# Attention's output product as four products on row halves of the array, in place of two block diagonal ones

## The chip, the cores and the metric

One core of one Trainium2 chip runs one program. TensorE (PE) multiplies, loading the stationary operand (PEld) and streaming the moving one; VectorE (DVE), ScalarE (ACT) and GpSimd (POOL) work beside it; SyncE (SP) issues DMAs. The metric is the device time of one execution in microseconds, as the median of several runs.

## The reference

Three parts follow each other; the output of one is the input of the next.

```python
# 1. attention over 32 memory slots: 4 batches, 8 heads, 576 tokens, 64 wide
a = softmax(phi, axis=2)                          # (4, 8, 576, 32)
k_m = einsum('bhsm,bhsd->bhmd', a, k)             # (4, 8, 32, 64)
v_m = einsum('bhsm,bhsd->bhmd', a, v)
attn = softmax(q @ k_m^T / 8, axis=-1)            # (4, 8, 576, 32)
x = (attn @ v_m) as (2304 tokens, 512)
# 2. mixture of 8 experts, two for each token
noisy = x @ w_gate + log1p(exp(x @ w_noise)) * noise
out = sum over a token's two experts of weight * (relu(x @ w1[e]) @ w2[e])   # 512 -> 1024 -> 512
# 3. two layers
h = out @ w_in                                    # 512 -> 2048
result = (h * cos(h)) @ w_out                     # 2048 -> 512
```

## The kernel before

**Attention.** The 2304 tokens are 18 tiles of 128 rows (`NT`). For each of the 4 batches `k_gen(b)` takes the softmax over phi, sums k and v into 32 slots a head (`kp`, L589), normalises them (`kd`, `vm`) and lays out two operands. `bdkt` holds the slot keys for the score product. `bdv` (L608) holds the slot values: for a group g of four heads, 128 rows (4 heads of 32 slots) and 272 columns. Columns 0 to 255 are block diagonal: head j's 64 values stand in columns 64 j to 64 j + 63 of its own 32 rows and the rest is zero, which POOL makes with the mask `bmask` (L612). Columns 256 to 271 are each slot's values times that head's rows of the two gate matrices (`pw`, L623, copied by ACT at L624). So one product gives a tile's attention output and its 16 gate logits (8 for the gate, 8 for the noise).

For each tile `t_gen(t)` computes the scores (`sc`, L659, PE), the softmax (`smx` and `sd` on DVE, the exponential on ACT, `ssm` on DVE, `d` on POOL), transposes `d` on PE (`pt`, L679), copies it to `e2T` on ACT (L681), and multiplies on PE (L689): for g = 0 and 1, `x[:, g, 0:272]`, one PSUM bank for each g. All operands are fp32; each such product is two records in the profile. ACT copies columns 0 to 255 of both banks to `xs` with a scale (L694) and columns 256 to 271 to the tile's place in `lgb` (L700), then makes the fp16 high part of `xs` (L704); POOL subtracts it for the low part (L705) and SP stores both (L706). There is one buffer for `x`, so a tile's product waits for ACT's copies of the tile before. A tile that spans two batches (tiles 4 and 13; `segs`) is computed in two halves of 64 tokens, each with its batch's operand.

**Routing.** Tiles 0 to 7 are group 0 and tiles 8 to 17 group 1. `route(g)` first adds the two partial logits of `lgb` (L349, DVE), then goes through noise, the two largest, ranks (`rank`, PE) and a table product (`tab`, L433, PE, behind the last tile's product x) to the row indices `idxA` (L438) and `idxB`. Steps of `route(0)` stand between the steps of tiles 12, 13, 14 and 17 in DVE's order; `route(1)` follows the last tile.

**Experts and last layers.** POOL gathers rows of x by `idxA` (L829), SP transposes them, and PE multiplies by w1 and w2 for the 8 experts and then by the last two layers: fp16 products `h`, `y`, `g`, `o`, from 106 us to the end. ACT and DVE scale the weights to fp16 high and low parts meanwhile, the first expert's already during the attention's end (`w`, `junk`, L219).

**Order.** Each step is put in a list with a time written by hand (`at`, `a_of(i) = 21 + 2.5 i`, `t_steps`, `k_steps`); a planner turns times into priorities and orders each engine's instructions by them and by a simulated timeline. Some places in the order are fixed by hand, as in

```python
AHEAD = (9, 10, 11, 13, 14, 15, 16)
with gated(f"t{ahead}T"):     # product x of tile t behind the transposes of tile t + 1 on PE
with gated(f"t{ahead}E"):     # copy of x of tile t behind the copy e2T of tile t + 1 on ACT
with gated(f"t{NT - 1}P"):    # table products behind the last product x
```

Of the kernel before, what the change touches and what calls it, by code (L numbers as in the profile page):

```python
# [9 lines left out]
F32 = mybir.dt.float32  # L10
# [4 lines left out]
AF = mybir.ActivationFunctionType  # L15
OP = mybir.AluOpType
AX = mybir.AxisListType
PSUM = bass.MemoryType.PSUM

P = 128  # L20
B, H, S, D, M = 4, 8, 576, 64, 32
# [3 lines left out]
E = 8  # L25
# [4 lines left out]
GROUPS = [(0, 8), (8, 18)]  # L30
# [30 lines left out]
def fused_kernel(ctx, tc, phiT, qT, kv, wgn, noise, w1, w2, wi, wo, out):  # L61
    nc = tc.nc
    V, A, G, T, SP = nc.vector, nc.scalar, nc.gpsimd, nc.tensor, nc.sync
# [15 lines left out]
    last = {}  # L79
# [25 lines left out]
    def sm(shape, dt, name):  # L105
        return small.tile(shape, dt, name=name)
# [32 lines left out]
    hp = sm([P, 1], F32, "hp")  # L139
    V.memset(hp, math.pi / 2)  # L140

    bmask = sm([P, 4], F32, "bmask")
    V.memset(bmask, 0.0)
    for j in range(4):
        V.memset(bmask[32 * j:32 * j + 32, j:j + 1], 1.0)
    wgn_sb = sm([64, H, 2 * E], F32, "wgn_sb")
    noise_sb = sm([P, NT, E], F32, "noise_sb")
    lgb = {}
    sT = sm([P, 2, NT], F32, "sT")
# [192 lines left out]
    def route(g):  # L342

        t0, t1 = GROUPS[g]
        n = t1 - t0
        ts = slice(t0, t1)
        u, w1p, l, c, y = (rg(g, k, n, E) for k in "uwlcy")
        lgp = rg(g, "lgp", n, 2 * E)
        V.tensor_tensor(lgp, lgb[g][:, :, 0], lgb[g][:, :, 1], op=OP.add)  # L349
        gate, z = lgp[:, :, 0:E], lgp[:, :, E:]  # L350
        last["u"] = V.scalar_tensor_tensor(u, z, -1.0, z, op0=OP.mult, op1=OP.max)
        A.activation(u, u, AF.Exp, scale=-1.0)
# [30 lines left out]
        d = rg(g, "d", n)  # L383
# [37 lines left out]
        for t in range(t0, t1, 3):  # L421
# [6 lines left out]
            for q in range(m):  # L428
                ohp = small.tile([P, 2, P], F16, tag="ohp", name="ohp", bufs=4)
                for k in range(2):  # L430
                    V.tensor_scalar(ohp[:, k], iota_r, pf[:, t + q, k:k + 1], None, op0=OP.is_equal)
                    with gated(f"t{NT - 1}P"):
                        last[f"tab{t + q - t0}"] = T.matmul(  # L433
                            tb[:, :nc_], lhsT=ohp[:, k], rhs=oha[:, q, k], start=(t + q == t0 and k == 0),
                            stop=(t + q == t1 - 1 and k == 1))
# [80 lines left out]
    ap = att.enter_context(tc.tile_pool(name="ap", bufs=2))  # L516
# [37 lines left out]
    def k_gen(b):  # L554
# [50 lines left out]
        last[f"bdk{b}V"] = V.tensor_copy(bk[0:64, :, 0:M], pv[0:64, :, 0, :])  # L605
        last[f"bdk{b}A"] = A.activation(bk[64:128, :, M:], pv[64:128, :, 1, :], AF.Copy)
        yield
        bv = ap.tile([P, 2, 272], F32, tag="bdv", name="bdv")  # L608
        bdv[b] = bv
        mb = bmask[:, :, None].to_broadcast([P, 4, D])  # L610
        for g in range(2):
            G.tensor_tensor(bv[:, g, 0:256].rearrange("p (j d) -> p j d", d=D),  # L612
                            vm[:, g, None, :].to_broadcast([P, 4, D]), mb, op=OP.mult)
        pv = trk("pv")
        for g in range(2):
            T.transpose(pv[0:64, g * P:(g + 1) * P], vm[:, g, :], ident)
# [4 lines left out]
        for h in range(H):  # L621
            r = slice(32 * (h % 4), 32 * (h % 4) + 32)
            T.matmul(pw[r, h // 4, :], lhsT=vt[:, h // 4, r], rhs=wgn_sb[:, h, :], start=True, stop=True)  # L623
        A.activation(bv[:, :, 256:272], pw, AF.Copy)  # L624
        yield
        vq = ap.tile([P, 1], F32, tag="vq", name="vq", bufs=1)
        sb = ap.tile([P, 2], F32, tag="sb", name="sb", bufs=1)
# [25 lines left out]
    def t_gen(t):  # L653

        sc = scb[:, t % 2]
        for p0, n, b in segs(t):
            c0 = (t % 8) * P + p0
            for c in range(4):
                T.matmul(sc[p0:p0 + n, 64 * c:64 * c + 64], lhsT=qt[t // 8][:, c, c0:c0 + n],  # L659
                         rhs=bdkt[b][:, c, :], start=True, stop=True)  # L660
        yield
        sv = sc.rearrange("p (h m) -> p h m", m=M)
        mx = ap.tile([P, H], F32, tag="smx", name="smx")
        V.tensor_reduce(mx, sv, axis=AX.X, op=OP.max)
        dk = sds[t % 4]
        dv = dk[:, :, 0:M]
        V.tensor_tensor(dv, sv, mx[:, :, None].to_broadcast([P, H, M]), op=OP.subtract)
        yield
        A.activation(dv, dv, AF.Exp, scale=0.125)
        yield  # L670
        su = ap.tile([P, H], F32, tag="ssm", name="ssm")
        V.tensor_reduce(su, dk, axis=AX.X, op=OP.add)
        last[f"t{t}V"] = V.reciprocal(su, su)
        d = ap.tile([P, 2 * P], F32, tag="d", name="d")
        G.tensor_tensor(d.rearrange("p (h m) -> p h m", m=M), dv, su[:, :, None].to_broadcast([P, H, M]), op=OP.mult)
        yield
        pt = ptb[:, t % 2]
        for g in range(2):
            last[f"t{t}T"] = T.transpose(pt[:, g * P:(g + 1) * P], d[:, g * P:(g + 1) * P], ident)  # L679
        eT = ap.tile([P, 2, P], F32, tag="e2T", name="e2T")  # L680
        last[f"t{t}E"] = A.activation(eT.rearrange("p g s -> p (g s)"), pt, AF.Copy)  # L681
        yield
        ahead = t + 1 if t in AHEAD else None
        x = aps.tile([P, 2, 512], F32, tag="x", name="x")
        with gated(f"t{ahead}T"):
            for p0, n, b in segs(t):
                pn = slice(p0, p0 + n)
                for g in range(2):
                    last[f"t{t}P"] = T.matmul(x[pn, g, 0:272], lhsT=eT[:, g, pn], rhs=bdv[b][:, g, :], start=True,  # L689
                                              stop=True)  # L690
        yield
        xs = l2k([P, DM], F32, "xs")
        with gated(f"t{ahead}E"):
            A.activation(xs.rearrange("p (g d) -> p g d", g=2), x[:, :, 0:256], AF.Copy,  # L694
                                          scale=sT[:, 0, t:t + 1])
        g = ROUTE_OF[t]
        if t == GROUPS[g][0]:
            n = GROUPS[g][1] - GROUPS[g][0]
            lgb[g] = rg(g, "lgb", n, 2, 2 * E)
        last[f"t{t}A"] = A.activation(lgb[g][:, t - GROUPS[g][0]], x[:, :, 256:272], AF.Copy)  # L700
        yield
        hl = l2k([P, 2 * DM], F16, "hl")
        hv = hl.rearrange("p (w d) -> p w d", w=2)
        A.activation(hv[:, 0], xs, AF.Copy)  # L704
        G.tensor_tensor(hv[:, 1], xs, hv[:, 0], op=OP.subtract)  # L705
        SP.dma_start(xd[t * P:(t + 1) * P, :], hl)  # L706
        yield
# [403 lines left out]
    x = X[0]  # L1111
# [161 lines left out]
```

## Time and profile before

| | |
|---|---|
| time of 3 runs | median 925.77 us (924.71 to 926.04) |
| profiled execution | 926.95 us, its span 925.1 us |
| PE, PEld busy | 879.5 us (95%), 511.0 us (55%) |
| DVE, ACT, POOL busy | 582.4 (63%), 467.7 (51%), 215.4 (23%) |
| mean granted clock of TensorE | 0.974 of 2.4 GHz |

Times are microseconds from the start of the span. Busy PE time is modelled and runs from a product's start to its last result, so products that follow each other overlap in it; intervals between starts tell more. In a timeline each row merges equal instructions that follow each other: start, time from the first start to the last end, engine, line, operation, output and inputs, the part of the array used and the shape, count, and in brackets the idle time of the engine before it with what ended it. `PEclk` 1.00 is 2.4 GHz and 0.50 is 1.2 GHz.

### The profile page before, as it was taken

The page shows a single profiled execution, that of the slowest core. Times are in us where ns is not written, and L with a number is a line of the kernel's source. Part 1 is how long each engine was busy: PE and PEld are TensorE (multiplying, and loading weights), DVE is VectorE, ACT ScalarE, POOL GpSimd, SP SyncE. Part 2 cuts the span into 40 slices and gives each one's busy share as a digit, 9 for nine tenths or more (in the row PEclk, how much of TensorE's full clock was granted, in tenths as well). Part 3 has the DMA queues.
Part 4 walks back from the last instruction along what each step waited for, and adds up shares of the span by engine and source line. Part 5 has one row for each costly group of instructions (what it writes and reads, how often), then busy time and mean ns, then how long its engine had stood idle before and what let it go on. Part 6 is the DMA issues. An engine that isn't in the chain of part 4 may idle for free. (4 is left out here: it accounts for less than half of the span.)

```text
span 925.1 us, 14179 instructions
## 1 busy us (share of the span) xinstructions
PE 879.5 (95%) x5368; PEld 511.0 (55%) x5368; DVE 582.4 (63%) x1266; ACT 467.7 (51%) x830; POOL 215.4 (23%) x234
## 2 busy tenths in 40 slices
PE   5997499999999999999999998999999999999997
PEld 4875355746566574756555565664444444444564
DVE  3668753766657575766571377787875765554564
ACT  3588426666666676777761334444333432422242
POOL 1355222110201101020000034434322521322221
PEclk9897599999999999999999999999999999999999
DMA  9982469787778979696762553322301610200010
GB/s 353 395 300 86 114 167 263 240 291 236 237 257 252 289 242 282 231 307 247 205 216 93 171 160 58 95 52 72 80 1 12 149 23 12 68 12 1 1 46 23
DMA packets 108246, 146.55 MB, mean 158 GB/s; under 512 B 65808, under 2 KB 66448, under 8 KB 106128
## 3 DMA queue, kind: packets, MB, share of 16 engines
q1 hardware_dynamic: 89536, 103.56, 36.5%
q0 software_dynamic: 6080, 19.93, 7.5%
q10 hardware_dynamic: 12560, 22.13, 6.7%
q8 instruction: 43, 0.70, 0.3%
q14 instruction: 27, 0.22, 0.1%
HBM read 95.26 MB, written 35.13 MB: 141 GB/s over the span
## 5 line engine op out<-in xcount | busy, mean ns | idle before, releaser
L219 PE MATMUL h<-x,w 128*128 128x384 f16 (+1 forms) x1536 | 215.3, 302 | 9.8 <-DMA x<-xg 9.2
L219 PE MATMUL y<-w,hT 128*128 128x512 f16 x960 | 210.7, 379 | 2.2 <-issue 2.2
L219 PE MATMUL g<-x2T,win 128*128 128x256 f16 (+1 forms) x1152 | 203.8, 327 | 5.5 <-DVE ty L1048 4.9
L219 PE MATMUL o<-wout,gT 128*128 128x512 f16 x864 | 202.5, 380 | 0.3 <-POOL gT L1050 0.2
L219 PEld LDWEIGHTS <-w 128*128 128x128 f16 x1536 | 151.5, 99 | 68.9 <-DMA x<-xg 8.8
L219 PEld LDWEIGHTS <-win 128*128 128x128 f16 x1152 | 113.2, 98 | 89.8 <-issue 6.8
L219 PEld LDWEIGHTS <-hT 128*128 128x128 f16 x960 | 93.9, 99 | 111.4 <-issue 2.7
L1050 POOL TENSOR_TENSOR gT<-ty,gT 128x256 f16<-128x256 f32 (+1 forms) x96 | 92.9, 968 | 253.8 <-ACT gT L1049 249.9
L1047 ACT ACTIVATE tt<-tt,hp 128x256 f32<-128x256 f32 (+1 forms) x96 | 58.9, 614 | 163.8 <-DVE tt L1046 147.7
L219 PEld LDWEIGHTS <-gT 128*128 128x128 f16 x864 | 84.4, 98 | 93.8 <-POOL gT L1050 1.9
L219 DVE SCALAR_TENSOR_TENSOR w<-raw,wsc,w 128x1024 f16<-128x1024 f32 x64 | 81.1, 1288 | 32.8 <-ACT w L219 31.2
L219 DVE SCALAR_TENSOR_TENSOR hT<-h,hT 128x384 f16<-128x384 f32 (+1 forms) x128 | 61.4, 487 | 61.9 <-ACT hT L219 61.7
L1044 DVE SCALAR_TENSOR_TENSOR ty<-g,wis,bct 128x256 f32<-128x256 f32 (+1 forms) x96 | 58.9, 613 | 65.1 <-PE g L219 65.1
L219 ACT ACTIVATE hT<-h 128x384 f16<-128x384 f32 (+1 forms) x128 | 55.2, 435 | 74.3 <-PE h L219 70.2
L1048 DVE SCALAR_TENSOR_TENSOR ty<-g,fac,tt 128x256 f32<-128x256 f32 (+1 forms) x96 | 59.1, 616 | 53.0 <-ACT tt L1047 52.5
L1049 ACT ACTIVATE gT<-ty 128x256 f16<-128x256 f32 (+1 forms) x96 | 50.2, 523 | 66.0 <-DVE ty L1048 65.9
L829 POOL DMA_INDIRECT xg<-xd,idxB x24 | 25.1, 1045 | 218.3 <-DMA x<-xg 206.9
L219 ACT ACTIVATE w<-raw,wsc 128x1024 f16<-128x1024 f32 x64 | 71.6, 1140 | 4.1 <-DVE wsc L219 1.9
L219 ACT ACTIVATE junk<-raw 128x1024 bf16<-128x1024 f32 x64 | 67.3, 1052 | 3.8 <-ACT o L219 2.5
L1046 DVE SCALAR_TENSOR_TENSOR tt<-tt,ty 128x256 f32<-128x256 f32 (+1 forms) x96 | 67.5, 703 | 2.6
L219 ACT ACTIVATE o<-y,ysc 128x512 f32<-128x512 f32 x40 | 27.5, 687 | 73.3 <-PE y L219 73.3
L968 POOL DMA_INDIRECT y<-yd,sidx x36 | 36.2, 1004 | 88.4 <-DMA yd<-o 80.7
(234 smaller groups left out, 712.8 us busy)
## 6 DMA issues: line engine op xcount, KB each, us to landing
raw<-in_w SPq DMA_DIRECT2D x32, 1024.0 KB, 11.4
yd<-o ACTq DMA_DIRECT2D x40, 256.0 KB, 6.8
kvt<-in_kv SPq DMA_DIRECT2D x9, 1024.0 KB
cvt<-in_wi SPq DMA_DIRECT2D x8, 1024.0 KB
wst<-cvt SPq DMA_DIRECT2D x16, 512.0 KB
cvt<-in_wo SPq DMA_DIRECT2D x8, 1024.0 KB, 8.6
yd<-zero ACTq DMA_DIRECT2D x13, 512.0 KB, 7.1
xd<-hl SPq DMA_DIRECT2D x18, 256.0 KB, 2.0
```

The costliest lines, as they stand in the source:

```text
L219: last[key] = fn(*a, **kw)
L829: G.indirect_dma_start(out=g, out_offset=None, in_=xd[0:NA * P] if part == 0 else xd, in_offset=bass.IndirectOffsetOnAxis(ap=idx[:, col:co ...
L968: G.indirect_dma_start(out=y, out_offset=None, in_=yd[0:rows], in_offset=bass.IndirectOffsetOnAxis(ap=sidx[:, t, k:k + 1], axis=0))
L1044: V.scalar_tensor_tensor(y, ph[:, :n], wis[:, 2 * E + c:2 * E + c + 1], bct[j], op0=OP.mult, op1=OP.mult)
L1046: V.scalar_tensor_tensor(t, t, MAGIC, y, op0=OP.subtract, op1=OP.subtract)
L1047: A.activation(t, t, AF.Sin, bias=hp, scale=-2.0 * math.pi)
L1048: V.scalar_tensor_tensor(y, ph[:, :n], fac[:, c:c + 1], t, op0=OP.mult, op1=OP.mult)
L1049: A.activation(g[:, 0, :n], y, AF.Copy)
L1050: G.tensor_tensor(g[:, 1, :n], y, g[:, 0, :n], op=OP.subtract)
```

## The change

The mask gets two columns in place of four, so that `bdv` has 128 + 16 = 144 columns: a head's values stand in the first or the second 64 columns by its number's parity. Rows 0 to 63 (heads 0 and 1 of the group) and rows 64 to 127 (heads 2 and 3) are then separate products of 64 rows: `x[:, j, 144 g : 144 g + 144]` for row half j, so that the two row halves of a group go to two PSUM banks and the two groups lie side by side in a bank. Each product gives 128 columns of x and a partial sum of the 16 logits. ACT's copy of x reads four pieces of 128 columns, its copy to `lgb` four pieces of 16, and `route` reduces four partial sums in place of adding two. `lgb` of group 0 moves to the attention's pool.

```diff
--- before.py
+++ after.py
@@ -139,10 +139,10 @@
     hp = sm([P, 1], F32, "hp")
     V.memset(hp, math.pi / 2)
 
-    bmask = sm([P, 4], F32, "bmask")
+    bmask = sm([P, 2], F32, "bmask")
     V.memset(bmask, 0.0)
     for j in range(4):
-        V.memset(bmask[32 * j:32 * j + 32, j:j + 1], 1.0)
+        V.memset(bmask[32 * j:32 * j + 32, j % 2:j % 2 + 1], 1.0)
     wgn_sb = sm([64, H, 2 * E], F32, "wgn_sb")
     noise_sb = sm([P, NT, E], F32, "noise_sb")
     lgb = {}
@@ -346,7 +346,7 @@
         ts = slice(t0, t1)
         u, w1p, l, c, y = (rg(g, k, n, E) for k in "uwlcy")
         lgp = rg(g, "lgp", n, 2 * E)
-        V.tensor_tensor(lgp, lgb[g][:, :, 0], lgb[g][:, :, 1], op=OP.add)
+        V.tensor_reduce(lgp, lgb[g].rearrange("p t s n -> p t n s"), axis=AX.X, op=OP.add)
         gate, z = lgp[:, :, 0:E], lgp[:, :, E:]
         last["u"] = V.scalar_tensor_tensor(u, z, -1.0, z, op0=OP.mult, op1=OP.max)
         A.activation(u, u, AF.Exp, scale=-1.0)
@@ -605,12 +605,12 @@
         last[f"bdk{b}V"] = V.tensor_copy(bk[0:64, :, 0:M], pv[0:64, :, 0, :])
         last[f"bdk{b}A"] = A.activation(bk[64:128, :, M:], pv[64:128, :, 1, :], AF.Copy)
         yield
-        bv = ap.tile([P, 2, 272], F32, tag="bdv", name="bdv")
+        bv = ap.tile([P, 2, 144], F32, tag="bdv", name="bdv")
         bdv[b] = bv
-        mb = bmask[:, :, None].to_broadcast([P, 4, D])
+        mb = bmask[:, :, None].to_broadcast([P, 2, D])
         for g in range(2):
-            G.tensor_tensor(bv[:, g, 0:256].rearrange("p (j d) -> p j d", d=D),
-                            vm[:, g, None, :].to_broadcast([P, 4, D]), mb, op=OP.mult)
+            G.tensor_tensor(bv[:, g, 0:128].rearrange("p (j d) -> p j d", d=D),
+                            vm[:, g, None, :].to_broadcast([P, 2, D]), mb, op=OP.mult)
         pv = trk("pv")
         for g in range(2):
             T.transpose(pv[0:64, g * P:(g + 1) * P], vm[:, g, :], ident)
@@ -621,7 +621,7 @@
         for h in range(H):
             r = slice(32 * (h % 4), 32 * (h % 4) + 32)
             T.matmul(pw[r, h // 4, :], lhsT=vt[:, h // 4, r], rhs=wgn_sb[:, h, :], start=True, stop=True)
-        A.activation(bv[:, :, 256:272], pw, AF.Copy)
+        A.activation(bv[:, :, 128:144], pw, AF.Copy)
         yield
         vq = ap.tile([P, 1], F32, tag="vq", name="vq", bufs=1)
         sb = ap.tile([P, 2], F32, tag="sb", name="sb", bufs=1)
@@ -686,18 +686,25 @@
             for p0, n, b in segs(t):
                 pn = slice(p0, p0 + n)
                 for g in range(2):
-                    last[f"t{t}P"] = T.matmul(x[pn, g, 0:272], lhsT=eT[:, g, pn], rhs=bdv[b][:, g, :], start=True,
-                                              stop=True)
+                    for j in range(2):
+                        pj = slice(64 * j, 64 * j + 64)
+                        last[f"t{t}P"] = T.matmul(x[pn, j, 144 * g:144 * g + 144], lhsT=eT[pj, g, pn],
+                                                  rhs=bdv[b][pj, g, :], start=True, stop=True)
         yield
         xs = l2k([P, DM], F32, "xs")
         with gated(f"t{ahead}E"):
-            A.activation(xs.rearrange("p (g d) -> p g d", g=2), x[:, :, 0:256], AF.Copy,
-                                          scale=sT[:, 0, t:t + 1])
+            xv = x[:, :, 0:288].rearrange("p j (g n) -> p g j n", g=2)
+            A.activation(xs.rearrange("p (g j d) -> p g j d", g=2, j=2), xv[:, :, :, 0:128], AF.Copy,
+                         scale=sT[:, 0, t:t + 1])
         g = ROUTE_OF[t]
         if t == GROUPS[g][0]:
             n = GROUPS[g][1] - GROUPS[g][0]
-            lgb[g] = rg(g, "lgb", n, 2, 2 * E)
-        last[f"t{t}A"] = A.activation(lgb[g][:, t - GROUPS[g][0]], x[:, :, 256:272], AF.Copy)
+            if g:
+                lgb[g] = rg(g, "lgb", n, 4, 2 * E)
+            else:
+                lgb[g] = ap.tile([P, n, 4, 2 * E], F32, name="lgb", bufs=1)
+        last[f"t{t}A"] = A.activation(lgb[g][:, t - GROUPS[g][0]].rearrange("p (g j) n -> p g j n", g=2),
+                                      xv[:, :, :, 128:144], AF.Copy)
         yield
         hl = l2k([P, 2 * DM], F16, "hl")
         hv = hl.rearrange("p (w d) -> p w d", w=2)
```

## Rows read from the trace of the kernel before

**Rows 1.** Busy time by stages: stretch, length, each engine's busy time (count), clock, DMA.
```profile
30.10:63.00 32.90, 32.71 (x388) 26.86 (x388) 20.29 (x64) 26.64 (x78) 16.49 (x22) 1.00 1.02 379
...
74.40:77.90 3.50, 2.68 (x19) 1.95 (x19) 3.47 (x18) 2.25 (x5) 1.43 (x2) 1.00 0.19 75
77.90:81.30 3.40, 1.72 (x10) 0.98 (x7) 3.30 (x12) 3.07 (x8) 2.07 (x3) 1.00 0.28 108
81.30:93.00 11.70, 8.20 (x29) 4.98 (x26) 7.98 (x34) 8.98 (x20) 5.83 (x6) 0.50 0.22 83
```

**Rows 2.** Timeline of PE around the product x of a whole tile.
```profile
31.28 0.38 PE L679 MATMUL pt<-ident,d 128*128 128x128 f32 x2
31.50 1.08 PE L689 MATMUL x<-bdv,e2T 128*128 128x272 f32 x4
32.42 0.38 PE L577 MATMUL et<-ident,ew 128*128 128x128 f32 x2
32.63 1.00 PE L659 MATMUL sc<-bdk,qt 128*128 128x64 f32 x8
33.48 0.83 PE L577 MATMUL et<-ident,ew 128*128 128x128 f32 x6
```

**Rows 3.** Timeline of PE around the product x of tile 4, in two halves.
```profile
46.30 0.39 PE L601 MATMUL pk<-ident,kd 128*128 128x128 f32 x2
46.61 1.14 PE L689 MATMUL x<-bdv,e2T 128*64 128x272 f32 x8
47.69 0.44 PE L679 MATMUL pt<-ident,d 128*128 128x128 f32 x2
47.96 0.38 PE L577 MATMUL et<-ident,ew 128*128 128x128 f32 x2
```

**Rows 4.** Waits of PE from 63 to 93 us: total, times, longest.
```profile
PE sc L659 <- DVE sd L667: 2.6, 3, 1.2
```

**Rows 5.** Timeline of PE at the attention's end.
```profile
84.19 2.02 PE L689 MATMUL x<-bdv,e2T 128*128 128x272 f32 x4
86.00 0.64 PE L679 MATMUL pt<-ident,d 128*128 128x128 f32 x2
87.13 2.18 PE L689 MATMUL x<-bdv,e2T 128*128 128x272 f32 x4 [0.50 <-ACT rt L700]
90.24 2.18 PE L689 MATMUL x<-bdv,e2T 128*128 128x272 f32 x4 [0.92 <-ACT rt L700]
92.22 0.47 PE L433 MATMUL tab<-oha,ohp 128*128 128x40 f16 x8
```

**Rows 6.** Timeline of ACT at the attention's end.
```profile
86.31 0.69 ACT L694 ACTIVATE xs<-x,sT 128x512 f32<-128x512 f32 x1 [0.97 <-PE x L689]
...
89.41 0.69 ACT L694 ACTIVATE xs<-x,sT 128x512 f32<-128x512 f32 x1 [0.51 <-PE x L689]
...
92.52 0.69 ACT L694 ACTIVATE xs<-x,sT 128x512 f32<-128x512 f32 x1 [0.78 <-PE tab L433]
...
94.22 0.63 ACT L704 ACTIVATE hl<-xs 128x512 f16<-128x512 f32 x1
```

**Rows 7.** Timeline of all engines, from the last tile to the first expert product.
```profile
94.98 1.16 POOL L705 TENSOR_TENSOR hl<-xs,hl 128x512 f16<-128x512 f32 x1 [1.96 <-issue]
...
96.31 1.93 POOL L829 DMA_INDIRECT xg<-xd,idxA  x1 [0.17 <-issue]
...
106.43 5.30 PE L219 MATMUL h<-x,w 128*128 128x256 f16 x24 [8.71 <-DMA x<-xg]
```

**Rows 8.** DVE's groups by form: busy time, mean ns, idle before.
```profile
L559 DVE TENSOR_REDUCE mx<-ph 128x2 f32<-128x1152 f32 x1 | 1.3, 1301 | 0.0
L349 DVE TENSOR_TENSOR rlgp<-rlgb 128x128 f32<-128x128 f32 x1 | 1.2, 1219 | 0.0
```

**Rows 9.** Timeline of DVE at the first index result.
```profile
94.37 0.31 DVE L349 TENSOR_TENSOR rt<-rt 128x160 f32<-128x160 f32 x1
...
95.30 0.17 DVE L438 TENSOR_SCALAR idxA<-tab 128x16 int32<-128x16 f32 x1 [0.23 <-PE tab L433]
```

## The prediction

> **What bounds the kernel now.** I read the busy table by stages first, then PE's timeline through the attention, then who waits for whom there, then ACT, DVE and POOL at the attention's end. The change touches only the first 95 us. From 30.1 to 63 us PE is busy 32.71 of 32.90 us at the full clock, with ACT at 26.64 and DVE at 20.29 [rows 1]: PE sets the pace, its products start back to back, and no wait of PE's is listed in that stretch. From 74.4 to 81.3 us DVE is busy 3.47 of 3.50 and 3.30 of 3.40 us while PE has slack [rows 1], and PE's score products wait for DVE's subtraction (2.6 us) [rows 4]: DVE sets the pace. From 81.3 to 93 us TensorE runs at its lower level, 1.2 GHz [rows 1], and the last tiles go round one loop: product x on PE, its copy by ACT out of the only x buffer, the next product x. ACT stands idle 0.97, 0.51 and 0.78 us ahead of the last three copies [rows 6], and the last two products start after idle times of 0.50 and 0.92 us ending at ACT's copy [rows 5]. What follows is a chain in series: ACT's fp16 copy of tile 17 at 94.22 [rows 6], POOL's difference at 94.98, the first gather of expert rows at 96.31, and the first expert product at 106.43, for which PE had waited 8.71 us [rows 7]. From there to the end PE is nearly always busy, so what the attention gives back moves the end by as much.
>
> **The product itself.** A full tile has four records of 272 columns (two fp32 passes for each of two products), from 31.50 to the next product's start at 32.42: 0.92 us, 229 ns each [rows 2]. After the change it has eight of 144 columns, 144/272 of 229 = 121 ns each. If the two row halves stream at once, that is four steps: 0.49 us, a saving of 0.43. If not, 0.97 us, a loss of 0.05. No product in this trace uses the rows 64 to 127 alone, so the overlap is not shown. The nearest row is the tile that spans two batches: its eight records of 272 columns, on two halves of the columns, take from 46.61 to 47.69, 1.08 us with its switches [rows 3], where one after the other they would take 8 x 0.229 = 1.83. So halves of the array do run at once, loads and all, and overlap is my value, with 0.97 us as the other end. Eight loads of 128 columns come with it: the score products of 64 columns, 32.63 to 33.48 = 0.85 us for eight records [rows 2], go at 0.106 us each where their streaming is 64/272 of 229 = 54 ns, so there the loads set the pace. The Trainium skill's page "TensorE: Matmul & The Clock Gate" says in its section LDWEIGHTS that a load's time goes by the columns and not by the rows, so that a half-row load saves nothing; by that alone, with loads in turn, the sum is the 926.3 of the first rival. The same page's Part 3 says that loads of different row groups overlap; by that it stays 921.8. The trace shows the first for whole-array loads (0.106 us) and nothing of two row groups.
>
> **The switch of tile form.** Two transposes, product x and the next two transposes take 31.28 to 32.63 = 1.35 us when all use the whole array [rows 2]; the same sequence around the split tile takes 46.30 to 47.96 = 1.66 us [rows 3]. Going into a divided array and back costs 0.31 us.
>
> **Stage A, 30 to 63 us, PE bound.** Nine products x lie here (40 records: eight full tiles, one split). Streaming gives 9 x 0.43 = 3.87 us. Switches: the products at 31.5, 51.1 and 61.0 stand between whole-array products and pay 0.31 each; the split tile pays already; the other five have a divided product (the k and v sums, or a split score product) on one side or on both, and pay between 0 and 0.31, which I take as 0.1 each, since one of their two switches is there already. Together 1.4 us, so -2.45 us if PE stays the bound. ACT with 26.64 us of work would then have 30.4 us, and a part will turn into waits for ACT and DVE, whose steps are in order: I take -1.7 (bounds -2.45 and 0). The halved mask products on POOL count nothing: POOL is busy 16.49 of 32.90 us there [rows 1].
>
> **Stage B, 63 to 84 us, DVE bound.** Product x is mostly beside DVE's work and its saving is hidden. DVE's sum of the gate partials changes: an addition of 128 elements that took 1219 ns becomes a reduction of 512. The reduction of 1152 elements took 1301 ns [rows 8], 1.13 ns an element, so 512 take 0.58: -0.6 us on the bounding engine. Bounds: if the 1219 ns was a delay that a reduction meets too, up to +0.4. ACT's gate copy grows from 32 to 64 elements in four pieces; at about 1 ns an element or less it is 0.03 a tile. I take -0.6 for the stage.
>
> **Stage C, the tail, 84 to 96 us.** Here product x is on the path, at the lower clock: 84.19 to the next start at 86.00 = 1.81 us [rows 5]. After: 4 x 0.24 = 0.97 and a switch, some 0.15 on the way in, so 0.69 less. Copy of tile 15: 0.69 earlier. Tile 16's product starts 0.69 earlier and is 0.69 shorter; its copy gains 1.29, as ACT's other work then stands in front of it. Tile 17's gains 2.0. The cap is ACT's idle time, 0.97 + 0.51 + 0.78 = 2.26 us [rows 6]; what is late next is ACT itself, with its weight scaling and squares in order. I take -2.0 (bounds -2.26 and +0.9, the latter with no overlap). The fp16 copy, POOL's difference and the gather all follow. The index table also needs PE's table products, which start when the last product x is done (92.22 [rows 5]): they move too. The second group's sum grows from an addition of 160 elements (0.31 us at 94.37) to a reduction of 640, about 0.72 us by the same rate, ahead of the index result at 95.30 [rows 9]; the index is then ready some 0.4 later, and POOL, held until 96.14 by its difference [rows 7], hides it; without that cover it costs 0.4.
>
> **Costs beside these.** With less work PE's clock may fall earlier. In the stretch after which it fell PE was busy 1.72 of 3.40 us, in the one before, after which it stayed, 2.68 of 3.50 [rows 1]. The latter loses about 0.5 and lies then between the two; what the clock does with that no row tells. A fall some 3 us earlier meets only one product x and one pair of transposes, with PE idle half the time: +0.2. The wider gate copy costs +0.1 on the tail. The first expert products ran at the lower clock from 106.43 on; where the rise falls after an earlier start is open, up to 1 us either way, taken as 0.
>
> **Sum.** -1.7 - 0.6 - 2.0 + 0.3 = -4.0 us. The profiled execution took 926.95 us (span 925.1), so 922.95 for its like; it lies 1.2 above the median of 925.77, and on that footing the forecast is 921.8.
>
> **Rivals.**
> *The loads bind.* If the loads of the two row halves wait for each other at the score products' 0.106 us, product x is 8 x 0.106 = 0.85 us at the full clock, against 0.92, and stage A becomes 9 x -0.07 + 1.4 = +0.8; at the lower clock eight loads of 0.21 make 1.7 against 1.81, about nothing with the switch; with stage B's -0.6 and +0.3 it is +0.5: 926.3. Against it: the split tile's loads overlapped. This is where the Trainium skill's section on LDWEIGHTS, weighed above, would lead.
>
> *The halves run one after the other* (the slower side). Each product is 0.97 us against 0.92 and still pays the switches: stage A 9 x 0.05 + 1.4 = +1.9; tail 3 x (0.13 + 0.15) = +0.8; with -0.6 and +0.1, +2.2: 928.0. It decides from the point at which a tile's eight records stretch over more than 0.92 us. For it: no row of this trace has two row halves at work; against it, the column halves.
>
> *The clock falls early and stays down.* If it fell at about 71 us in place of 81.3, three tiles' scores, transposes and products would run at half speed, each tile some 1.5 us longer (score products 0.85, transposes 0.2 [rows 2], product x 0.45), 4.5 in all, of which PE's idle time from 74.4 to 81.3, 0.82 + 1.68 = 2.5 us [rows 1], hides the greater part: +2, so -2 in all: 923.8. If it fell in stage A, where PE has no slack, each 3 us at half speed would cost 1.5, and the gain would be gone: about 926. For it: PE has less to do in every tile. Against it: in stage A its other products stand back to back.
>
> **How the numbers follow.** Forecast 0.60; clock early 0.17 (two thirds of it in stage B); loads bind 0.12; one after the other 0.11. A difference under 0.2% (1.85 us) can't be told from none here. Faster by more: 0.56 of the forecast, 0.09 of the clock's case and 0.02 of the loads' with a better tail, 0.67. Slower by more: 0.08 of the last case, 0.03 of the clock's, 0.02 of the loads', 0.13. The same: 0.20. The range: below, all of stage A (-2.45), 0.6 more in stage B, the cap in the tail and 1 us from the clock's rise give -6.6, 919.2; above, the loads' case and half of the serial case, +1.5: 927.3. The likeliest case's own range is 919.2 to 923.8.
>
> **What would show it.** Product x's records in pairs a few ns apart, a pair each 0.12 us, and 0.5 us from the first start to the last stream's end; a gap of about 0.2 us to the neighbours. Stage A shorter by 1 to 2.5 us with PE still near full. The gate sum at about 0.6 us. ACT's idle ahead of the last three copies nearly gone, the first gather at 91.5 to 93 us in place of 96.31, the first expert product as much earlier. Eight records evenly spaced by 0.106 or 0.121 would show the rivals; a lower clock well ahead of 78 us the third. The prediction is wrong if the first expert product moves by less than 2 us, or moves and the end doesn't follow.

## The result, and the profile after

The changed kernel takes 931.74 us as the median of 4 runs, the kernel before 925.9 us beside it: the ratio is 1.0059 (95% interval 1.0043 to 1.0075), some 5.5 us slower, where 921.8 was forecast and a range up to 927.3. The profiled span is 929.3 us against 925.1, the mean granted clock 0.970 against 0.974.

The operation itself did what the forecast said. PE's timeline around product x of a whole tile, after, which answers to [rows 2]:

```profile
30.14 0.38 PE L679 MATMUL pt<-ident,d 128*128 128x128 f32 x2
30.45 0.76 PE L691 MATMUL x<-bdv,e2T 64*128 64x144 f32 x8
31.14 0.44 PE L577 MATMUL et<-ident,ew 128*128 128x128 f32 x2
31.41 1.00 PE L659 MATMUL sc<-bdk,qt 128*128 128x64 f32 x8
```

From product x to the next product's start it is 0.69 us in place of 0.92: the two row halves run at once (one after the other would be 0.97). Two transposes, product x and the next two transposes take 1.27 us in place of 1.35, so what product x gains is nearly all lost again around it (0.08 us is left of the 0.43 that the streaming alone would save).

The windows of the stages after (stretch, length, busy time of PE, PEld, DVE, ACT, POOL with counts, clock, DMA), against [rows 1]:

```profile
30.10:63.00 32.90, 30.35 (x413) 24.22 (x411) 19.54 (x62) 26.94 (x78) 16.32 (x23) 1.00 1.02 385
...
74.40:77.90 3.50, 3.19 (x17) 2.80 (x18) 3.36 (x17) 2.10 (x6) 1.50 (x2) 0.50 0.03 7
77.90:81.30 3.40, 3.40 (x31) 3.04 (x29) 2.71 (x11) 2.93 (x6) 1.10 (x3) 0.50 0.20 80
81.30:93.00 11.70, 7.59 (x42) 5.63 (x38) 6.48 (x27) 8.64 (x18) 6.05 (x7) 0.50 0.17 68
```

PE has slack in the first stretch now (its 413 records hold 80 of product x in place of 40), and the lower clock stands already at 74.4. The loss comes after this stretch. PE's waits from 63 to 99 us (total, times, longest) name it:

```profile
PE pt L679 <- POOL d L675: 4.6, 2, 3.6
PE sc L659 <- DVE sd L667: 2.5, 2, 2.2
```

The transposes of tile 17 wait 3.6 us for its probabilities `d`, and these for DVE. DVE's timeline after, the steps ahead of that tile's maximum (`smx`, L664), and its wait at the end:

```profile
83.27 0.72 DVE L425 TENSOR_TENSOR oha<-acode,af 128x240 f16<-128x240 f16 x2
...
83.98 1.79 DVE L431 TENSOR_SCALAR ohp<-iota_r,pf 128x128 f16<-128x128 f16 x5
85.70 0.40 DVE L427 TENSOR_TENSOR oha<-oha,tokb 128x240 f16<-128x240 f16 x1
86.02 0.57 DVE L431 TENSOR_SCALAR ohp<-iota_r,pf 128x128 f16<-128x128 f16 x3
86.50 0.40 DVE L427 TENSOR_TENSOR oha<-oha,tokb 128x240 f16<-128x240 f16 x1
...
86.90 0.41 DVE L664 TENSOR_REDUCE smx<-sc 128x8 f32<-128x256 f32 x1
```

One-hot steps of the first routing (L425 to L431) stand ahead of the maximum of the last tile, and what they feed, the table products, waits on PE behind the last product x anyway. DVE's waits in the same stretch:

```profile
DVE ohp L431 <- PE tab L433: 6.4, 1, 6.4
```

Before, the same maximum ran at 78.25 us and the one-hot steps came behind it:

```profile
78.25 0.41 DVE L664 TENSOR_REDUCE smx<-sc 128x8 f32<-128x256 f32 x1
```

Maxima 14, 15 and 16 are late too, at 73.77, 77.17 and 80.44 us in place of 68.86, 70.96 and 74.77; from 69.13 to 73.77 routing steps and the scale's copies stand ahead of maximum 14. What follows on PE, against [rows 5]:

```profile
85.95 1.33 PE L691 MATMUL x<-bdv,e2T 64*128 64x144 f32 x8 [0.34 <-ACT rt L706]
90.92 0.69 PE L679 MATMUL pt<-ident,d 128*128 128x128 f32 x2 [3.63 <-POOL d L675]
91.54 1.33 PE L691 MATMUL x<-bdv,e2T 64*128 64x144 f32 x8
93.83 1.33 PE L691 MATMUL x<-bdv,e2T 64*128 64x144 f32 x8 [0.96 <-ACT rt L706]
```

and at the index result, the first gather and the first expert product, against [rows 7, 9]:

```profile
97.83 1.24 DVE L349 TENSOR_REDUCE rt<-rt 128x160 f32<-128x640 f32 x1
...
99.68 0.17 DVE L438 TENSOR_SCALAR idxA<-tab 128x16 int32<-128x16 f32 x1 [0.23 <-PE tab L433]
...
100.14 2.01 POOL L836 DMA_INDIRECT xg<-xd,idxA  x1 [1.21 <-DVE tabB L439]
...
110.24 5.05 PE L219 MATMUL h<-x,w 128*128 128x256 f16 x24 [8.81 <-DMA x<-xg]
```

Product x of tile 17 is 1.33 us long in place of 2.18, but starts 3.6 us late; the gather is 3.8 us late and the first expert product as much. And the gather now waits for DVE's `tabB` (1.21 us), no longer for POOL.

### The profile page after: what moved, and what is told of

It reads as the page before. It is cut to its first block, busy times and chain, and to the rows that moved or that the text cites. A ratio compares the mean times of both kernels' runs of the same rounds, so it can differ in the third digit from the quotient of the medians.

```text
span 929.3 us, 14331 instructions
## 1 busy us (share of the span) xinstructions
PE 877.8 (94%) x5448; PEld 511.2 (55%) x5448; DVE 582.0 (63%) x1266; ACT 468.2 (50%) x830; POOL 213.1 (23%) x234
## 5 line engine op out<-in xcount | busy, mean ns | idle before, releaser
L219 ACT ACTIVATE w<-raw,wsc 128x1024 f16<-128x1024 f32 x64 | 71.6, 1139 | 4.1 <-ACT o L219 2.1
```

What stands on the lines that cost most here:

```text
L219: last[key] = fn(*a, **kw)
```

## The experiments

The theory: the operations gain, and the loss is the order of instructions, which the planner made anew because it counts the four products one after another. The rivals: the operations' side costs (sums, copies, switches), and the clock. Ratios are to the kernel before on the same chip, with 95% intervals; the last columns are from the profile of one execution each. These executions do not reach the attention at the same time: product x of tile 0 starts at 30.00 us in e10 and at 32.47 in e4, which are equal up to there, since equal products ahead of it run at half the pace in different stretches (48 records of `kp` at 13 us take 1.52 us in e10 and 2.79 in e4). So the gathers of two runs are compared below from a common event, not by the column. In e2 the clock rose again at about 80 us and fell at about 90.

| run | ratio | first gather (us) | clock fell at (us) |
|---|---|---|---|
| before / after | 1 / 1.0059 | 96.31 / 100.14 | 81.3 / 74.0 |
| e1 before's order | 0.9971 (0.9960 to 0.9982) | 95.19 | 70.4 |
| e2 after's order, old products | 1.0069 (1.0056 to 1.0082) | 100.51 | 73.0 |
| e3 DVE's order alone | 1.0000 (0.9990 to 1.0009) | 96.41 | 71.5 |
| e4 = e1, sum behind the index | 0.9945 (0.9932 to 0.9959) | 94.98 | 68.8 |
| e5 = e1 with added products | 0.9963 (0.9949 to 0.9977) | 94.61 | 81.8 |
| e6 = e4 and e5 | 0.9942 (0.9925 to 0.9959) | 93.48 | 81.2 |
| e7 gates two tiles later | 1.0031 (1.0018 to 1.0044) | 101.19 | 65.4 |
| e8 two products of 288 | 0.9998 (0.9986 to 1.0009) | 95.85 | 71.6 |
| e9 = e1, scalings behind gathers | 0.9957 (0.9943 to 0.9971) | 94.83 | 67.9 |
| e10 = e4, scalings beside gather | 0.9957 (0.9940 to 0.9974) | 93.77 | 62.4 |
| e11 = e6, scalings behind gathers | 0.9956 (0.9940 to 0.9971) | 92.38 | 79.8 |
| e12 last gate | 1.0034 (1.0022 to 1.0045) | 97.39 | 69.5 |

**The order, exchanged between the two kernels (e1, e2, e3).** Every instruction, from the start to among the first expert's products, is tied to its predecessor on its engine in a given order, without a semaphore; the products x of a tile are one entry.

```diff
+    ORDER = {"PE": "0 4 1-3 5-53 ... x0 158 162 ...", "DVE": ..., ...}   # places in before's order
+    def pin():
...
+        for a, b in zip(seq, seq[1:]):
+            tc.add_manual_dep(b, a.name, NoSync, reason="pin")
...
+    at(tA + 0.75, pin)
```

e1 does this to the changed kernel with the order of before on all engines, e3 on DVE alone; e2 to the kernel before with the order of after.

> The changed kernel's operations, with every engine's order of instructions up to the first expert product fixed to that of the kernel before (the four products stand where the two stood). Order theory (the loss comes from steps of the first routing that the planner put on DVE ahead of the maxima of tiles 14 to 17, because it counts the four products one after the other): the last product x starts at 87 to 89 us in place of 93.8, the first expert product at 103 to 106 in place of 110.2, time 921 to 925 us. Rival, the operations themselves (switches of tile form, dearer sums, wider copies): the order changes little, 929 to 932 us. Rival, the clock: TensorE's lower clock again begins at about 74 us as PE has less to do, and eats half of the gain: 926 to 929 us.

> The mirror image: the operations of the kernel before (two block diagonal products of 272 columns), in the order of instructions of the changed kernel on every engine. Order theory: slower than the changed kernel (931.7), since it has the bad order and no faster products: 932 to 937 us, with maximum 17 on DVE near 87 to 90 us. Operations theory: about the kernel before, 925 to 928 us.

> The changed kernel with DVE's order alone fixed to that of the kernel before; the planner orders the other engines anew. If DVE's order is the cause, most of the loss goes: 921 to 926 us. If PE's and ACT's new order has a share of its own, it stays between: 927 to 930 us. If order is not the cause: 931 to 933 us.

Measured: 923.76, 932.53 and 926.67 us. The order theory holds in both directions: the same operations go from 1.0059 to 0.9971 (0.88%, about 8 us), and the old products in the new order are as slow as the new ones. The operations are worth 0.3% in the old order and nothing that can be told in the new one. The clock does not make the difference: it fell at 70.4 us in e1, earlier than in the changed kernel (74.0). e3 lies between the ranges that it was given (921 to 926, 927 to 930 us): DVE's order alone gives back 0.59% of the 0.88%, and the rest is the order of the other engines. One place of it can be read on PE: the scores of tile 17 (`sc`) stand ahead of product x of tile 13 in e1 and behind it in e3. PE's timeline of e1, then of e3:

```profile
77.12 1.81 PE L720 MATMUL sc<-bdk,qt 128*128 128x64 f32 x8
78.86 1.25 PE L752 MATMUL x<-bdv,e2T 64*64 64x144 f32 x16
```

```profile
76.72 1.25 PE L729 MATMUL x<-bdv,e2T 64*64 64x144 f32 x16
77.90 1.97 PE L697 MATMUL sc<-bdk,qt 128*128 128x64 f32 x8
```

Maximum 17 is at 79.15 in e1 and at 79.91 in e3, and the routing steps, in order behind it on DVE, follow: the index result comes at 94.72 and at 95.94, though e3's last product x is 0.85 us earlier (88.03 against 88.88). Counted from product x of tile 1 (36.71 in e1, where the clock rose late, 35.35 in e3), e3's maximum 17 is 2.1 us late and its index result 2.6. What ACT's and POOL's order add to this was not taken apart.

**What turns the planner (e8, e7, e12).** e8 lets the planner order freely, but shows it two products a tile:

```diff
-                for g in range(2):
-                    for j in range(2):
-                        pj = slice(64 * j, 64 * j + 64)
-                        ... T.matmul(x[pn, j, 144 * g:144 * g + 144], lhsT=eT[pj, g, pn], rhs=bdv[b][pj, g, :])
+                for j in range(2):
+                    pj = slice(64 * j, 64 * j + 64)
+                    ... T.matmul(x[pn, j, 0:288], lhsT=eT[pj, 0, pn], rhs=bdv[b][pj] (both g))
```

> The changed kernel in the planner's own order, but a tile's output product written as two products of 64 rows and 288 columns (one for each row half, both column halves at once) in place of four of 144: the chip streams the same columns, the planner sees two products. The scores of the second group of heads are left out (the first group's stand in for them), so it is a probe and no version to use. If the planner orders badly because it counts four products one after another, it goes back to nearly the order of before, maximum 17 on DVE stands at 80 us or earlier in place of 86.9, and the time is 922 to 926 us. Rival: something else of the change (the dearer sums, the copies) turns the order: 929 to 932 us.

The probe leaves out the second group's scores. Measured 926.46 us, a little above the expected span. Product x takes as long as with four (31.78 to the next start at 32.46), and the last maximum is back at its old place:

```profile
31.78 0.76 PE L690 MATMUL x<-bdv,e2T 64*128 64x288 f32 x4
32.46 0.44 PE L577 MATMUL et<-ident,ew 128*128 128x128 f32 x2
```

```profile
78.41 0.42 DVE L664 TENSOR_REDUCE smx<-sc 128x8 f32<-128x256 f32 x1 [0.21 <-PE sc L659]
```

The dearer sums and copies are still in it, so most of the turn in the order (0.61% of the 0.88%) comes with the number of products that the planner sees. That it adds their durations up is the natural reading; no run shows its own timeline. e8 is not back at e1 (0.9998 against 0.9971, the intervals apart): whether the sums and copies turn that last part is open.

e7 and e12 mend the order by the gates that the kernel has:

```diff
-    for t, n in ((12, 7), (13, 7), (14, 6)):
+    for t, n in ((14, 7), (15, 7), (16, 6)):      # e7 only
...
-    at(a_of(17) + 7.25, advance, r0, 99, "t16V", lead=7.0)
+    at(a_of(17) + 7.25, advance, r0, 99, "t17V", lead=7.0)   # e7 and e12
```

> The changed kernel (931.7 us) in the planner's own order, with two lines of gates changed: the steps of the first routing may be issued only behind the softmax sums of tiles 14, 15, 16 and 17 in place of 12, 13, 14 and 16. Order theory: maxima 14 and 15 no longer stand behind routing steps on DVE, most of the 8 us between this order and that of the kernel before comes back: 925 to 928 us. Rival: steps held back end up behind the last tile, so that the index result is as late as now: 930 to 933 us.

> The changed kernel (931.7 us) in the planner's own order, with one word changed: the last part of the first routing (its one-hot steps among it, 3.6 us on DVE from 83.3 to 86.8, ahead of maximum 17 at 86.90) may be issued only behind the softmax sum of tile 17 in place of tile 16. Order theory: maximum 17 at 83.5 to 84 us, tile 17's transposes at about 87.8 in place of 90.9, the last product x at 90.4 to 90.9 in place of 93.8, the first gather about 3.1 us earlier, time 927.8 to 929.5 us: this one place is then some two fifths of the 8 us that the order costs, the rest being routing steps ahead of maxima 14 to 16. Rival: the one-hot steps only change places, and the index result comes as late as now: 930.5 to 932.5 us.

e12 (929.13 us) goes nearly as written (its last product x is 0.2 us past the range, its gather 2.75 us earlier than after in place of 3.1): DVE, PE and POOL of e12:

```profile
83.85 0.42 DVE L664 TENSOR_REDUCE smx<-sc 128x8 f32<-128x256 f32 x1 [1.24 <-PE sc L659]
```

```profile
87.44 0.66 PE L679 MATMUL pt<-ident,d 128*128 128x128 f32 x2
88.56 1.33 PE L691 MATMUL x<-bdv,e2T 64*128 64x144 f32 x8 [0.46 <-ACT rt L706]
91.08 1.33 PE L691 MATMUL x<-bdv,e2T 64*128 64x144 f32 x8 [1.19 <-ACT rt L706]
```

```profile
97.39 2.02 POOL L836 DMA_INDIRECT xg<-xd,idxA  x1 [1.21 <-DVE tabB L439]
```

One word in a gate gives back 0.25% of the 0.88%, by intervals that just touch. e7 (928.51 us) is a miss of half a microsecond and cannot be told from e12. Steps held back longer are late themselves: in e7's profile maximum 17 stands at 87.12 us, and the one-hot steps come only at 91.03 (e12: 86.70, after: 83.27). That execution took 930.52 us, 2 us above e7's median, with the clock down from 65.4, so how much of this is the gates is not shown.

**The index path (e4).** In e1 the copy of tile 17 is 2.2 us earlier than before [rows 6], but the gather only 1.1, since the sum stands on the path. e4 moves it.

```diff
-    "... 198-201 210 197 211 202-203 208-209 277 ..."    # DVE: 210 the sum, 202-203 idxA and tabB
+    "... 198-201 197 202-203 210-211 208-209 277 ..."
```

> The changed operations in the order of the kernel before (923.8 us), with one edit: the second group's sum of gate partials (1.23 us on DVE, right ahead of the last one-hot product, the last table product and the index result idxA) and the operation after it stand behind idxA and tabB. Theory that the index path on DVE sets the first gather (POOL waits 1.21 us for tabB there): idxA 1.3 us earlier, the gather at 93.9 to 94.2 us in place of 95.2, bound then by POOL's difference, and the time 922.5 to 923.0 us. Rival, as the prediction had it (POOL's difference hides the sum): nothing, 923.5 to 924.2 us. Second rival: the second routing comes later by as much and is waited for: 924 to 925.5 us.

All engines at that place, e1:

```profile
92.88 1.23 DVE L410 TENSOR_REDUCE rt<-rt 128x160 f32<-128x640 f32 x1
...
94.72 0.18 DVE L499 TENSOR_SCALAR idxA<-tab 128x16 int32<-128x16 f32 x1 [0.23 <-PE tab L494]
...
94.91 3.67 DVE L280 SCALAR_TENSOR_TENSOR w<-raw,wsc,w 128x1024 f16<-128x1024 f32 x3
95.19 2.01 POOL L898 DMA_INDIRECT xg<-xd,idxA  x1 [1.21 <-DVE tabB L500]
97.51 1.89 POOL L898 DMA_INDIRECT xg<-xd,idxA  x1 [0.30 <-issue]
...
105.22 4.19 PE L280 MATMUL h<-x,w 128*128 128x256 f16 x24 [8.74 <-DMA x<-xg]
```

and e4:

```profile
94.18 0.17 DVE L499 TENSOR_SCALAR idxA<-tab 128x16 int32<-128x16 f32 x1 [0.38 <-PE tab L494]
...
94.36 1.21 DVE L410 TENSOR_REDUCE rt<-rt 128x160 f32<-128x640 f32 x1
94.98 1.15 POOL L898 DMA_INDIRECT xg<-xd,idxA  x1 [0.18 <-issue]
...
95.77 3.67 DVE L280 SCALAR_TENSOR_TENSOR w<-raw,wsc,w 128x1024 f16<-128x1024 f32 x3
96.44 1.42 POOL L898 DMA_INDIRECT xg<-xd,idxA  x1 [0.30 <-issue]
...
103.37 4.19 PE L280 MATMUL h<-x,w 128*128 128x256 f16 x24 [5.54 <-DMA x<-xg]
```

921.87 us, 0.26% below e1 by the ratios, twice what was expected. Counted from the last product x (88.88 and 89.48) the index is 1.1 us earlier, as expected, the gather 0.8, and POOL again sets it (0.18 in place of 1.21 us of wait); the first expert product is 2.45 us earlier. The rest fits the gathers: 2.01 + 1.89 us beside DVE's scalings `w`, 1.15 + 1.42 here.

**The gathers beside DVE (e9, e10, e11).** e9 and e10 take the two causes apart, e11 joins all.

```diff
 e9  "... 210 197 211 202-203 212-219 208-209 277-282 220-227 ..."    # sum ahead, scalings 208-209, 277-281 behind
 e10 "... 197 202-203 208-209 210-211 277 212 ..."                    # sum behind, scalings 208-209 ahead of it
 e11 "... 197 202-203 210-219 208-209 277-282 220-227 ..."            # with the added products of e5
```

> The kernel with the order of before (923.8 us; its gathers took 2.01 and 1.89 us on POOL beside DVE's weight scalings w, and 1.15 and 1.42 us in the kernel with the sum behind the index, where the sum stood beside the first). Here the sum stays ahead of the index, and DVE's weight scalings are put behind eight small operations of the second routing, so that the gathers run beside those. Theory that DVE's scalings slow the gather's issue on POOL: the two gathers take 0.95 to 1.2 us each, the first expert product comes about 1.5 us earlier than 105.2, time 922.0 to 922.8 us. Rival (the gathers are shorter for another reason, the time came from the index alone): gathers still near 2 us, time 923.5 to 925 us.

> The fourth corner: the sum behind the index, but two of DVE's weight scalings straight behind the index and ahead of the sum, beside the first gather. Theory that the scalings slow the gather: the first gather takes about 2 us again, the index is as early as without them, and the time is 922.5 to 923.3 us, between 921.9 (sum beside the gather) and 923.8 (sum ahead of the index). Rival (the index alone counts): 921.5 to 922.3 us.

> All that helped: the changed operations in the order of before, the sum behind the index, the added products after tiles 8 to 13 that keep the clock, and DVE's weight scalings behind both gathers. With 920.9 us for the first three, and about 0.4 us more off the second gather (1.42 to 0.95 us): 920.0 to 921.0 us. If the weights of the first expert then come too late: 921.5 to 924 us.

POOL's two gathers in e9 and, behind them, in e10, with DVE's rows beside e10's:

```profile
94.83 1.21 POOL L898 DMA_INDIRECT xg<-xd,idxA  x1 [1.21 <-DVE rt L415]
96.34 0.95 POOL L898 DMA_INDIRECT xg<-xd,idxA  x1 [0.30 <-issue]
```

```profile
93.14 2.73 DVE L280 SCALAR_TENSOR_TENSOR w<-raw,wsc,w 128x1024 f16<-128x1024 f32 x2
93.77 1.93 POOL L898 DMA_INDIRECT xg<-xd,idxA  x1 [0.18 <-issue]
95.80 1.21 DVE L410 TENSOR_REDUCE rt<-rt 128x160 f32<-128x640 f32 x1
96.00 0.95 POOL L898 DMA_INDIRECT xg<-xd,idxA  x1 [0.30 <-issue]
```

The rows settle that `w` lengthens a gather: it takes 1.4 to 2.0 us beside `w` (1.42 for e4's second, which no run explains), 0.95 beside the sum (e10's second), and 0.95 to 1.2 beside small operations (both of e9). From the last product x (88.88 us in e1, 88.53 in e9, 88.27 in e10) the first expert product comes 16.34 us later in e1, 14.76 in e9 and 14.41 in e10. In time e4, e9 and e10 (921.87, 922.89, 922.35 us) overlap and cannot be ranked, and the intervals of e9 and e10 overlap e1's as well.

e11 (921.89) misses its range. Its first expert product is 1.3 us earlier than e6's (100.68 against 101.96), but 1.1 of this is there at the last product x (86.88 against 87.98), and 1.2 at product x of tile 0, ahead of anything in which the two differ. Counted from the last product x it is 0.2 us earlier, and the first product of the second expert matrix (115.88 against 116.46) 0.5 us later. In between PE's `rank` of the second routing waits 0.50 us for DVE's `m` in e11 and not in e6: DVE's routing steps and scalings, put in another order, are waited for elsewhere. ACT too waits 7.33 us for `wsc` there (1.9 in e6).

**The clock (e5, e6).** Products that nobody reads keep PE as busy as before:

```diff
+            if t in range(8, 14):
+                for j in range(8):
+                    pj = slice(64 * (j % 2), 64 * (j % 2) + 64)
+                    T.matmul(x[:, j % 2, 384:512], lhsT=ident[pj, :], rhs=ident[pj, :], ...)
```

> The changed operations in the order of the kernel before (923.8 us), with products added whose result nothing reads: after product x of tiles 8 to 13, eight of 128 columns on the two row halves (about 0.45 us of PE a tile at the full clock), so that PE is as busy as it was in the kernel before. Clock theory (the shorter product lets TensorE's clock fall at 70 us in place of 81, and tiles 12 to 15 lose 1.5 to 2 us by it): the lower clock begins at 77 us or later, product x of tile 14 stands at 80 us or earlier in place of 81.2, and the time is 922 to 923 us. Rival: PE's time is not what binds there, or the added products cost what the clock gives: 923.5 to 926 us.

> Both edits of the two kernels before this one: the sum behind the index and the added products. If both theories hold, their gains add: 921 to 922 us. If only the index path holds: 922.5 to 924 us. If neither: 923.5 to 926 us.

Two windows of e1, then of e5:

```profile
63.00:70.40 7.40, 5.05 (x67) 4.29 (x68) 5.87 (x15) 7.38 (x21) 4.91 (x6) 1.00 0.23 89
70.40:74.40 4.00, 4.00 (x25) 3.71 (x23) 3.88 (x12) 3.19 (x10) 2.05 (x3) 0.52 0.20 70
```

```profile
63.00:70.40 7.40, 7.19 (x104) 6.62 (x104) 5.59 (x14) 7.25 (x20) 4.51 (x6) 1.00 0.25 94
70.40:74.40 4.00, 4.00 (x51) 3.70 (x51) 3.88 (x15) 3.23 (x10) 1.74 (x2) 1.00 0.21 83
```

The clock stays up to 81.8 us, and product x of tile 14 stands at 79.55 in place of 81.22, but tile 15's only at 83.48 against 83.93: in between PE waits 2.38 us for DVE's routing step `m`. Times are 923.32 us, 0.3 past the range of its theory, and 920.89; by the ratios e5 gains 0.08% on e1 and e6 0.03% on e4, nothing that can be told. This does not make the early fall free, since the added products cost PE time themselves. Up to the index the pinned runs have the same operations and order, the added products apart. From product x of tile 8 to that of tile 10, and to that of tile 15 (us):

| run | clock fell at | 8 to 10 | 8 to 15 |
|---|---|---|---|
| before | 81.3 | 6.93 | 23.15 |
| e1 | 70.4 | 7.05 | 23.34 |
| e4 | 68.8 | 7.05 | 24.36 |
| e9 | 67.9 | 7.06 | 24.33 |
| e10 | 62.4 | 8.77 | 25.53 |
| e5, e6, e11 (added products) | 81.8, 81.2, 79.8 | 7.96, 7.97, 7.96 | 24.11, 24.10, 24.10 |

The added products cost 0.9 us by tile 10, while the clock is still up in e1, e4 and e9. Without them a fall at 70.4 costs about 0.1 us up to tile 15, one at 67.9 or 68.8 about 1.1 and one at 62.4 about 2.3, an estimate from one execution each against 24.11 - 0.9 = 23.2. So the early fall is real, its price hangs on when it comes, which differs between executions, and the added products pay back about what they cost. By their medians e6 and e4 are the fastest versions, 0.58 and 0.55% below the kernel before and some 1.1 to 1.2% below the changed one; e9 to e11 overlap them.

## Why the prediction was wrong, step by step

**The step that failed** is one that was left unsaid: each step of the sum took DVE's work in the order of before and moved it earlier. Stage B said "Product x is mostly beside DVE's work and its saving is hidden"; what happened is that DVE's work was ordered anew. That costs about 8 us by e1 against after, and no rival named it, though the kernel's order is a planner's output and the change doubles the number of products that it plans with. The three rivals asked about the product's loads, its halves and the clock; it was none of these.

With the order restored the sum can be read term by term, from e5, whose clock rises and falls as before's does:

- *Stage A, -1.7:* product x of tile 0 to that of tile 8 takes 31.62 to 59.37 = 27.75 us, before 31.50 to 61.04 = 29.54. Measured -1.8. Right.
- *Stage B, -0.6:* tile 8 to tile 15 takes 24.11 us (to 83.48), before 23.15 (to 84.19): +1.0. The added products are 0.9 of it by the table above; the rest, about +0.1, stands against the -0.6. The first sum did get shorter (0.99 us in place of 1.22, where 0.58 was estimated), but 0.2 us on the engine that sets the pace did not show in the stage.
- *Stage C, -2.0:* product x of tile 15 to the end of tile 17's takes 83.48 to 89.63 = 6.15 us, before 84.19 to 92.42 = 8.23. Measured -2.1. Right.
- *The second sum, "POOL, held until 96.14 by its difference [rows 7], hides it":* wrong. From the end of the last product x to the gather it is 89.63 to 94.61 = 4.98 us, before 3.89: +1.1. The sum took 1.23 us, not 0.72, and once the copy came 2 us earlier POOL's cover was gone; the index path on DVE was next. The bound "without that cover it costs 0.4" stood in the text and was too small as well: from the end of the last product x the index came 1.6 us later than before (4.51 against 2.88), 0.9 of it by the sum. Another 0.6 stands in four of DVE's one-hot steps ahead of it (1.64 us in place of 1.04), which in e5 run beside the whole of POOL's difference of tile 16 (89.94 to 91.12); that they wait for it was not tested.

-1.8 + 1.0 - 2.1 + 1.1 is -1.8 us at the gather, against -4.0 forecast for the end; e5's span is 2.3 us shorter than before's. So in the old order too the forecast asked too much: it lacked the second sum's 1.1 us and stage B's 0.7. With the sum off the path (e4) the change is worth 5 us, a part of which is the shorter gathers and not the product.

*The rivals.* The halves do not run one after the other and the loads do not bind: 0.69 us. That eight loads and four cost the same (e8) speaks against a limit by loads too. The Trainium skill's page "TensorE: Matmul & The Clock Gate", Part 3, says that a load overlaps the products under way when its row group is another; the 0.69 us agree with it. The clock fell early, as the third rival said: at 74.0 us in the changed kernel, and between 62.4 and 70.4 in the old order, at 0.1 to 2.3 us by the table above, against the 2 that the rival gave. It is not what made the change slower, since e1 has it too.

## What to carry to other kernels

Where a planner orders the instructions, a change of their number or length is a change of the whole order: compare the two orders engine by engine before arguing about a nanosecond of the operation, and pin the old order to measure the new operation. A step that is hidden behind another engine has a cover of fixed length; when the same change shortens that engine's path, price the step without its cover. On an engine that works in order, work whose result is gated behind later work does harm by standing early. And two profiles are compared from a common event: here two executions of the same instructions reached product x of tile 0 2.5 us apart.

## What was not expected of the hardware

A gather of rows by index, issued by POOL, took 1.4 to 2.0 us beside DVE's weight scalings (`w`, two operands from SBUF), and 0.95 to 1.2 beside a reduction of 640 elements or small DVE operations; e10 shows 1.93 beside `w` and 0.95 beside the reduction in one run. The Trainium skill's page "SBUF — State Buffer", section "Who interferes with whom", says that a DVE instruction with two SBUF inputs contends with a GpSimd instruction that reads SBUF, and that a reduction doesn't; the rows agree with both.

Eight fp32 records on two row halves with a load each take 0.76 us busy and 0.69 to the next start, four records of twice the columns the same: the number of loads does not set that time. Of the 0.69 us, 0.2 is more than the 0.49 of streaming; that this is the change of tile form is argued from [rows 2] and [rows 3], not taken apart by a run.
